# Attention's steps as one chain behind fixed products, its VectorE operations behind the unit's sums, its matmuls behind the last product

## The chip, the core and the metric

The kernel runs on one core of one Trainium2 chip. TensorE (PE) does the matmuls, VectorE (DVE), ScalarE (ACT) and GpSimd (POOL) the elementwise work, and SyncE (SP) issues the DMAs. The metric is the device time of the whole program in microseconds, as the median of several runs.

## The reference

Eight batches, eight heads, 576 tokens, head size 64. Each head has 32 packing queries p. First the packing queries attend to the keys and values, which gives 32 packed vectors per head; then every token's query attends to these, which serve as keys and values at once:

```
def sm_attn(qq, kk, vv):
    s = scale * np.matmul(qq, kk.transpose(0, 1, 3, 2))
    s = s - np.max(s, axis=-1, keepdims=True)
    a = np.exp(s)
    a = a / (np.sum(a, axis=-1, keepdims=True) + 1e-09)
    return np.matmul(a, vv)
p_packed = sm_attn(p, k, v)
out = sm_attn(q, p_packed, p_packed)
```

The result, 4608 tokens by 512, goes through four experts, all of which are computed for all tokens and weighted by the normalised domain probabilities:

```
p = domain_probs / (domain_probs.sum(-1, keepdims=True) + 1e-09)
for e in range(E):
    h = np.maximum(x @ w1[e], 0.0)       # 512 -> 1024
    out += p[:, e:e + 1] * (h @ w2[e])   # 1024 -> 512
```

## The kernel before

**Units.** The work of the experts is cut into 64 units: a super-block of two batches, one of eight chunks (512 hidden columns of an expert) and one of the two batches. A pair of units is the two batches of one chunk. The second layer of a unit is one Winograd form of a 2 x 2 block product: seven products instead of eight, in the order `ORDER` = a11, s3, s1, s2, a22, s4, a12, called products 0 to 6. Each product is 12 matmuls of 128 x 288 in float32r, since every operand is split into a high part (a cast on ScalarE, L102) and a low part (a subtraction, L107), and is added to an accumulator by VectorE (L420).

**First layer of the next unit.** The four blocks of hidden values of the next unit are made between the products of the current one: `mm1_group` (L294), 12 matmuls each, a11 behind product 1, a22 behind product 3, a21 behind product 4 and a12 behind product 6. VectorE then applies relu and the probability (L322) and forms the sums (L319): for a21 the operand s3, a sum in place, the operand s2, and ScalarE's copy s1 (L331); for a12 the operand s4, and ScalarE's and VectorE's split of a12 itself (stl). The other operands are split by ScalarE (hi) and GpSimd (lo) into tiles named st. These operations are called the sums below.

**x is never formed.** Instead, `g_form` (L259) multiplies the packed vectors (ppbd) by w1 once per chunk and super-block, 32 matmuls in every even unit behind products 2 and 3, and mm1_group multiplies the result (ghl) by the attention weights of the tokens (xh, xl).

**Attention** of the next super-block's two batches runs between the products of this one, in generators that do one step at each place given by `slots`. `pack_unit` (L139), once per half g of the heads: load k; load v; scores (32 matmuls into two tiles, issued together), maximum nb (L166, L167), exp on ScalarE (L170), its sum's reciprocal rs (L175, L176); then for each batch five transposes (L70) with ScalarE copies, 40 matmuls with v, the scaling ppn (L199), a transpose of ppn and its copies into ppbd. `tok_unit` (L212), once per g: load q; scores; transposes of the scores on VectorE (L225); for each batch maximum (L230), subtraction (L231), exp (L232), then sum (L235), 1e-9 (L236), reciprocal (L237), multiplication (L238), then transpose (L241) and split. `AT_FIRST` (super-block 0) and `AT_LATER` say at which unit of the super-block each of the four generators starts, and `slots` behind which products a step is taken: 0, 2, 4 and 6, or 0, 2 and 5 for the token side of super-block 0.

**What sets the order.** All matmuls of the kind above write to one pool of four tiles in PSUM, ps_dbl (two banks each, name dbl); a tile is free again when the last reader is done. Matmuls issued `together` (scores, g_form) are a fixed point in TensorE's order: all before stand before, all after stand after. Among everything else the tile framework's scheduler chooses the order on each engine from a simulation of the program as it is recorded. The engines then work their lists in order. The w2 operands (tt) are formed in super-block 0 from rw tiles by ScalarE and GpSimd (L393, t_form) and stored to DRAM, and are loaded from there later. The last super-block has no attention beside it.

## Time and profile before

| | |
|---|---|
| Median of 3 runs | 1309.03 us (1308.78 to 1310.23) |
| The profiled execution | 1306.86 us, of which its span 1304.8 us |
| TensorE busy | 1255.7 us, 96% |
| VectorE busy | 917.5 us, 70% |
| GpSimd busy | 732.6 us, 56% |
| ScalarE busy | 501.8 us, 38% |

The profiled execution is one run of its own, and the span begins and ends with the first and last instruction seen in it, so it is 2.06 us shorter than that run's time. A busy share is an average over a program with an opening, three super-blocks with attention and one without. In a timeline a row shows start and length of an instruction (or of several of one kind), its engine, line and operation, and in brackets how long the engine had been idle and what ended that; matmuls are pipelined, so rows overlap a little and a product of 12 shows 1.74 us where products follow each other every 1.58 us.

### The profile page before, as it was taken

Reading aid. Unit: us, or ns where it says so; the run is one execution under the profiler, and the core shown is the slowest. Engines: PE = TensorE matmul, PEld = TensorE weight load, DVE = VectorE, ACT = ScalarE, POOL = GpSimd, SP = SyncE. Lnnn points to the kernel's source line nnn. Section 1 sums busy time; section 2 is a strip of 40 time slices with the busy share of each in tenths; the row PEclk is TensorE's granted clock in tenths of the full one; section 3 lists DMA queues with packets and bytes.
Section 4 is the critical chain, followed back from the end, with each engine's and each line's share of the span. In section 5 each row is a group of like instructions: output and inputs, shape, how many; then the busy total and the mean of one; then the engine's idle time right before and its main releaser. Section 6 shows DMA issues by size and latency. Waiting matters only on the chain.

```text
span 1304.8 us, 26845 instructions
## 1 busy us (share of the span) xinstructions
PE 1255.7 (96%) x10720; PEld 1173.2 (90%) x10720; DVE 917.5 (70%) x1384; ACT 501.8 (38%) x841; POOL 732.6 (56%) x531
## 2 busy tenths in 40 slices
PE   5989998998999999999999999999999999999997
PEld 2879888898999989999999898999999999999997
DVE  6565666878784666887786566798678467766677
ACT  2444434344435333333334433343333543333331
POOL 4877768588774433445556443445546554345545
PEclk9999999999999999999999999999999999999999
DMA  9665656345455446454345644344445443345422
GB/s 340 235 230 181 223 200 219 127 165 198 155 195 171 151 135 191 160 175 139 121 143 184 208 143 153 127 154 155 140 138 192 150 137 122 126 155 155 123 65 74
DMA packets 86219, 213.71 MB, mean 164 GB/s; under 512 B 8784, under 2 KB 27344, under 8 KB 86096
## 3 DMA queue, kind: packets, MB, share of 16 engines
q1 hardware_dynamic: 85424, 211.85, 49.0%
q8 instruction: 86, 1.41, 0.4%
q14 instruction: 37, 0.30, 0.1%
q10 hardware_dynamic: 672, 0.15, 0.1%
HBM read 173.09 MB, written 38.87 MB: 162 GB/s over the span
## 4 chain that ended last, share of the span: by engine, by line
PE 83%; POOL 6%; DVE 4%; issue 2%; DMA 2%; ACT 2%; POOLq 0%; SPq 0%; DVEq 0%; ACTq 0%
PE dbl L67 78%; PE dbl L75 5%; POOL st L107 3%; POOL acc L470 1%; POOL tt L107 1%; DVE ghl L107 1%; PE dbl L70 1%; DMA wraw<-in_w 1%; ACT ghl L102 1%; DMA vt<-in_v 1%; DVE sblk L319 0%; DMA rw<-in_w 0%; DVE acc L435 0%; DVE acc L420 0%; DVE nb L166 0%
## 5 line engine op out<-in xcount | busy, mean ns | idle before, releaser
L67 PE MATMUL dbl<-st,tt 128*128 128x288 f32 x4608 | 669.3, 297 | 14.3 <-POOL st L107 9.3
L67 PEld LDWEIGHTS dbl<-st,tt 128*128 128x128 f32 x4608 | 625.3, 188 | 49.2 <-issue 26.5
L107 POOL TENSOR_TENSOR st<-sblk,st 128x576 fp32r<-128x576 f32 x256 | 371.9, 1463 | 426.6 <-ACT st L102 425.0
L67 PE MATMUL dbl<-xh,ghl 128*128 128x288 f32 x2048 | 416.3, 296 | 0.0
L420 DVE TENSOR_TENSOR acc<-dbl,acc 128x576 f32<-128x576 f32 x385 | 289.0, 751 | 103.0 <-PE dbl L67 101.9
L67 PEld LDWEIGHTS dbl<-xh,ghl 128*128 128x128 f32 x2048 | 331.0, 190 | 0.2 <-DVE ghl L107 0.2
L67 PE MATMUL dbl<-xl,ghl 128*128 128x288 f32 x1024 | 304.2, 297 | 6.8 <-POOL xl L107 5.3
L102 ACT CAST st<-sblk 128x576 fp32r<-128x576 f32 x256 | 166.5, 674 | 301.3 <-DVE sblk L319 232.1
L107 POOL TENSOR_TENSOR st<-ablk,st 128x576 fp32r<-128x576 f32 x128 | 184.2, 1439 | 64.9 <-ACT st L102 58.6
L67 PEld LDWEIGHTS dbl<-xl,ghl 128*128 128x128 f32 x1024 | 194.5, 190 | 9.4 <-POOL xl L107 6.0
L322 DVE SCALAR_TENSOR_TENSOR dbl<-dbl,pbt 128x576 f32<-128x576 f32 x128 | 97.9, 765 | 81.7 <-PE dbl L67 75.3
L102 ACT CAST st<-ablk 128x576 fp32r<-128x576 f32 x128 | 86.3, 674 | 159.1 <-PE dbl L67 141.4
L322 DVE SCALAR_TENSOR_TENSOR ablk<-dbl,pbt 128x576 f32<-128x576 f32 x128 | 96.5, 754 | 71.0 <-PE dbl L67 70.6
L67 PE MATMUL dbl<-stl,tt 128*128 128x288 f32 x768 | 114.6, 299 | 10.3 <-ACT sblk L331 8.8
L107 DVE TENSOR_TENSOR ghl<-dbl,ghl 128x512 fp32r<-128x512 f32 x128 | 85.4, 687 | 54.7 <-ACT ghl L102 54.7
L67 PEld LDWEIGHTS dbl<-stl,tt 128*128 128x128 f32 x768 | 106.7, 191 | 11.6 <-ACT sblk L331 9.7
L102 ACT CAST ghl<-dbl 128x512 fp32r<-128x512 f32 x128 | 72.0, 589 | 61.0 <-DVE ghl L107 47.5
L107 POOL TENSOR_TENSOR tt<-rw,tt 128x512 fp32r<-128x512 f32 x56 | 74.8, 1349 | 19.1 <-ACT tt L102 19.1
L75 PE MATMUL dbl<-wraw,ppbd 64*32 64x512 f32 x1024 | 68.2, 601 | 2.2 <-DMA wraw<-in_w 2.2
L107 DVE TENSOR_TENSOR stl<-dbl,stl 128x576 fp32r<-128x576 f32 x64 | 48.2, 754 | 30.6 <-ACT stl L102 30.4
L331 ACT COPY sblk<-dbl 128x576 f32<-128x576 f32 x64 | 41.0, 641 | 73.6 <-DVE sblk L319 65.7
L470 POOL TENSOR_TENSOR acc<-acc,acc 128x576 f32<-128x576 f32 x28 | 39.9, 1435 | 30.2 <-DVE acc L420 30.2
(65 smaller groups left out, 686.1 us busy)
## 6 DMA issues: line engine op xcount, KB each, us to landing
tt<-td SPq DMA_DIRECT2D x175, 512.0 KB, 4.1
wraw<-in_w SPq DMA_DIRECT2D x132, 256.0 KB, 3.7
td<-tt SPq DMA_DIRECT2D x56, 512.0 KB, 5.2
pbt<-pnd SPq DMA_DIRECT2D x32, 288.0 KB, 4.0
out<-acc SPq DMA_DIRECT2D x32, 288.0 KB, 2.6
rw<-in_w SPq DMA_DIRECT2D x16, 512.0 KB, 5.0
kt<-in_k SPq DMA_DIRECT2D x14, 576.0 KB, 4.7
kt<-in_q SPq DMA_DIRECT2D x14, 576.0 KB, 6.6
```

What stands on the lines that cost most here:

```text
L67: on_pe(nc.tensor.matmul(**kw))
L70: on_pe(nc.tensor.transpose(**kw))
L75: ins = nc.tensor.matmul(**kw).ins
L102: nc.scalar.copy(out=dst, in_=src)
L107: eng.tensor_tensor(out=dst, in0=src, in1=hi.bitcast(F32), op=ALU.subtract)
L322: nc.vector.scalar_tensor_tensor(out=held(name) if c == kh else psv, in0=psv, scalar=0.0, in1=pbt[b][:, ts].rearrange("p (o t) -> p o t", ...
L331: nc.scalar.copy(out=held("s1"), in_=psv)
L420: nc.vector.tensor_tensor(out=accs[b, i], in0=psv, in1=accs[b, i], op=ALU.add)
L470: eng.tensor_tensor(out=m[dst], in0=m[x], in1=m[y], op=op)
```

## The change

A small class `Behind` wraps VectorE. What goes through `vec` (the unit's sums, the split of a12, the final combination) is remembered as the last sum; what goes through `avec` (all of attention's VectorE operations) gets a dependency that keeps it behind the last sum recorded so far, in the order on the engine alone, with no semaphore. The accumulations (L420 before, L441 after) and the splits of ghl are not wrapped. In the same way `product` remembers its last matmul, and every matmul recorded later is kept behind it. Both hold from unit 1 on. The two tables are replaced by `pair_attention`, one chain of both pack units and both token units, each with a free place behind its loads, started at unit 4 of super-block 0 and unit 1 of a later one, counted from 0; a step stands behind products 0, 2 and 5 in odd units and 0, 3 and 5 in even ones. Line numbers of the changed kernel: L67 becomes L87, L75 L95, L70 L90, L107 L127, and all wrapped operations show the line of the wrapper, L68.

The diff, without the places where only nc.vector becomes vec or avec in the same way:

```
@@ -58,9 +58,29 @@
     def after(ins, prev):
         tc.add_manual_dep(ins, prev.name, nosync, reason="order on TensorE")
 
+    class Behind:
+
+        def __init__(self, eng, key):
+            self.eng, self.key, self.on = eng, key, False
+
+        def __getattr__(self, op):
+            def issue(*args, **kw):
+                res = getattr(self.eng, op)(*args, **kw)
+                if self.key is None:
+                    order["sum"] = res.ins
+                elif self.on and order["sum"] is not None:
+                    after(res.ins, order["sum"])
+                return res
+            return issue
+
+    order["sum"], order["product"] = None, None
+    vec, avec = Behind(nc.vector, None), Behind(nc.vector, "sum")
+
     def on_pe(res):
         if order["last"] is not None:
             after(res.ins, order["last"])
+        if avec.on and order["product"] is not None:
+            after(res.ins, order["product"])
         order["free"].append(res.ins)
 
     def mm(**kw):
@@ -163,8 +183,8 @@
         a1s, rss = {}, {}
         for b in bs:
             nb = small.tile([P, 1], F32, name="nb")
-            nc.vector.tensor_reduce(out=nb, in_=pss[b][:, :, 0:HS], axis=AX.XY, op=ALU.max)
-            nc.vector.tensor_scalar_mul(nb, nb, -SCALE)
+            avec.tensor_reduce(out=nb, in_=pss[b][:, :, 0:HS], axis=AX.XY, op=ALU.max)
+            avec.tensor_scalar_mul(nb, nb, -SCALE)
             a1s[b] = new(b, [P, S], "a1")
             sm = small.tile([P, 1], F32, name="sm")
             nc.scalar.activation(
...
@@ -222,23 +242,23 @@
             a2s[b] = new(b, [P, S // 32, NPK], "a1")
             a2f = a2s[b].rearrange("p a n -> p (a n)")
             for c in range(2):
-                nc.vector.transpose(out=a2f[:, c * HS:(c + 1) * HS], in_=pss[b][:, c, 0:HS])
+                avec.transpose(out=a2f[:, c * HS:(c + 1) * HS], in_=pss[b][:, c, 0:HS])
         yield
         for b in bs:
             a2 = a2s[b]
             m2 = small.tile([P, S // 32, 1], F32, name="m2")
-            nc.vector.tensor_reduce(out=m2, in_=a2, axis=AX.X, op=ALU.max)
+            avec.tensor_reduce(out=m2, in_=a2, axis=AX.X, op=ALU.max)
...
@@ -316,10 +336,10 @@
             return blocks[u, name]
 
         def add(dst, x, y, op):
-            nc.vector.tensor_tensor(out=dst, in0=x, in1=y, op=op)
+            vec.tensor_tensor(out=dst, in0=x, in1=y, op=op)
 
         name = f"a{c + 1}{kh + 1}"
-        nc.vector.scalar_tensor_tensor(
+        vec.scalar_tensor_tensor(
             out=held(name) if c == kh else psv, in0=psv, scalar=0.0,
             in1=pbt[b][:, ts].rearrange("p (o t) -> p o t", o=1).broadcast_to([P, 2, HS]),
             op0=ALU.max, op1=ALU.mult,
@@ -412,6 +432,7 @@
                         start=n == 0, stop=n == 5,
                     )
                     n += 1
+        order["product"] = order["free"][-1]
         psv = ps[:, :, 0:HS]
         if (b, i) not in accs:
             accs[b, i] = apool.tile([P, 2, HS], F32, name=f"acc{i}")
...
@@ -489,6 +510,16 @@
         for gen in gens:
             yield from gen
 
+    def pair_attention(pair):
+        for make in (pack_unit, tok_unit):
+            for g in range(NG):
+                gen = make(pair, g, att_tile)
+                next(gen)
+                if make is pack_unit:
+                    next(gen)
+                yield
+                yield from gen
+
     def drain(gen):
         for _ in gen:
             pass
...
@@ -566,13 +597,11 @@
     nothing = iter(())
     GROUPS = {1: ((0, 0),), 3: ((1, 1),), 4: ((0, 1),), 6: ((1, 0),)}
     GROUPS_LATE = {3: ((0, 0),), 4: ((1, 1),), 5: ((0, 1),), 6: ((1, 0),)}
-    AT_FIRST = ((4, pack_unit, 0), (6, pack_unit, 1), (8, tok_unit, 0), (11, tok_unit, 1))
-    AT_LATER = ((1, pack_unit, 0), (4, pack_unit, 1), (7, tok_unit, 0), (9, tok_unit, 1))
     FORM = {0: (0, 2, 3, 4, 5, 6), 2: (6,), 3: (0, 1, 2, 3, 4)}
     for kh in range(2):
         w2_load(1, kh, raw_tile)
     tsteps = nothing
-    sums, back, slots = nothing, second_batch(), (0, 1, 2, 3, 4, 5, 6)
+    sums, back = nothing, second_batch()
     for u, (sb, ch, b) in enumerate(units):
         pos = u % (2 * NCH)
         odd = pos % 2 == 1
@@ -581,13 +610,11 @@
 
         if u == 1:
             drain(back)
-        if sb + 1 < SB:
-            pair = [2 * sb + 2, 2 * sb + 3]
-            for at_step, make, g in AT_FIRST if sb == 0 else AT_LATER:
-                if at_step == pos:
-                    drain(back)
-                    back = make(pair, g, att_tile)
-                    slots = (0, 2, 5) if sb == 0 and make is tok_unit else (0, 2, 4, 6)
+            avec.on = True
+        if sb + 1 < SB and pos == (4 if sb == 0 else 1):
+            drain(back)
+            back = pair_attention([2 * sb + 2, 2 * sb + 3])
+        slots = range(NPROD) if u == 0 else (0, 2, 5) if odd else (0, 3, 5)
 
         gsteps, gat = nothing, (2, 3)
         nsb, nch = (sb, ch + 1) if ch + 1 < NCH else (sb + 1, 0)
```

**VectorE, the second scores of super-block 1.** Unit 20, before. nb belongs to attention's pack unit; SCALAR_TENSOR_TENSOR is relu with the probability, here of a21; sblk are s3 and s2; acc are accumulations.

```order
L322 SCALAR_TENSOR_TENSOR dbl<-dbl,pbt 128x2x288
L319 TENSOR_TENSOR sblk<-ablk,dbl 128x576
L319 TENSOR_TENSOR dbl<-dbl,ablk 128x2x288
L166 TENSOR_REDUCE nb<-dbl 128x1 x2
L319 TENSOR_TENSOR sblk<-dbl,ablk 128x576
L167 TENSOR_SCALAR nb<-nb 128x1 x2
L420 TENSOR_TENSOR acc_4835<-dbl,acc_4835 128x576
L175 TENSOR_SCALAR rs<-sm 128x1
L176 RECIPROCAL rs<-rs 128x1
L175 TENSOR_SCALAR rs<-sm 128x1
L176 RECIPROCAL rs<-rs 128x1
L420 TENSOR_TENSOR acc_4855<-dbl,acc_4855 128x576
```

Afterwards, at the same scores:

```order
L68 SCALAR_TENSOR_TENSOR dbl<-dbl,pbt 128x2x288
L68 TENSOR_TENSOR sblk<-ablk,dbl 128x576
L68 TENSOR_TENSOR dbl<-dbl,ablk 128x2x288
L441 TENSOR_TENSOR acc_5097<-dbl,acc_5097 128x576
L68 TENSOR_TENSOR sblk<-dbl,ablk 128x576
L441 TENSOR_TENSOR acc_5126<-dbl,acc_5126 128x576
L68 SCALAR_TENSOR_TENSOR dbl<-dbl,pbt 128x2x288
L68 TENSOR_TENSOR sblk<-dbl,sblk 128x576
L441 TENSOR_TENSOR acc_4660<-dbl,acc_4660 128x576
L68 TENSOR_TENSOR stl<-dbl,stl 128x2x288
L68 TENSOR_REDUCE nb<-dbl 128x1 x2
L68 TENSOR_SCALAR nb<-nb 128x1 x2
```

The maximum nb, which stood between the sums of a21, now stands behind the sums of a21 and of a12, with stl the last of them.

**TensorE, the same scores.** Before: kt is the operand of the scores, xl and xh those of the group a21, st and stl those of products 5 and 6.

```order
L67 MATMUL dbl<-xl_2773,ghl 128x288
L67 MATMUL dbl<-xh_2772,ghl 128x288 x2
L75 MATMUL dbl<-kt,pt 32x288 x16
L67 MATMUL dbl<-st,tt 128x288 x12
L67 MATMUL dbl<-stl,tt 128x288 x12
L67 MATMUL dbl<-xl_2773,ghl 128x288
L67 MATMUL dbl<-xh_2772,ghl 128x288 x2
```

Afterwards:

```order
L87 MATMUL dbl<-xl_3065,ghl 128x288
L87 MATMUL dbl<-xh_3064,ghl 128x288 x2
L87 MATMUL dbl<-st,tt 128x288 x12
L95 MATMUL dbl<-kt,pt 32x288 x16
L87 MATMUL dbl<-st,tt 128x288 x12
L87 MATMUL dbl<-xl_3069,ghl 128x288
L87 MATMUL dbl<-xh_3068,ghl 128x288 x2
```

In unit 20 the scores stood between group a21 (of unit 21) and product 5; now they stand between products 0 and 1, which follow group a12 of unit 20 itself.

**VectorE, the token side in super-block 0.** Before: a, s and at are attention's (two batches, a_2874 and a_2877), the others the unit's.

```order
L235 TENSOR_REDUCE s_3047<-a_2874 128x18
L322 SCALAR_TENSOR_TENSOR dbl<-dbl,pbt 128x2x288
L235 TENSOR_REDUCE s_3263<-a_2877 128x18
L420 TENSOR_TENSOR acc_838<-dbl,acc_838 128x576
L236 TENSOR_SCALAR s_3047<-s_3047 128x18
L319 TENSOR_TENSOR sblk<-ablk,dbl 128x576
L319 TENSOR_TENSOR dbl<-dbl,ablk 128x2x288
L236 TENSOR_SCALAR s_3263<-s_3263 128x18
L420 TENSOR_TENSOR acc_870<-dbl,acc_870 128x576
L237 RECIPROCAL s_3047<-s_3047 128x18
L322 SCALAR_TENSOR_TENSOR dbl<-dbl,pbt 128x2x288
L319 TENSOR_TENSOR sblk<-dbl,ablk 128x576
```

Afterwards:

```order
L68 TENSOR_REDUCE s_3369<-a_3185 128x18
L441 TENSOR_TENSOR acc_790<-dbl,acc_790 128x576
L68 TENSOR_SCALAR s_3369<-s_3369 128x18
L68 RECIPROCAL s_3369<-s_3369 128x18
L68 TENSOR_TENSOR a_3185<-a_3185,s_3369 128x576
L68 SCALAR_TENSOR_TENSOR dbl<-dbl,pbt 128x2x288
L68 TENSOR_TENSOR sblk<-ablk,dbl 128x576
L68 TENSOR_TENSOR dbl<-dbl,ablk 128x2x288
L441 TENSOR_TENSOR acc_838<-dbl,acc_838 128x576
L68 TENSOR_TENSOR sblk<-dbl,ablk 128x576
L68 STREAM_TRANSPOSE at<-a_3185 128x576
L441 TENSOR_TENSOR acc_870<-dbl,acc_870 128x576
```

Small operations of two batches stood between the unit's sums; now one batch's operations stand in a row ahead of a group's sums or behind them.

## Rows read from the trace of the kernel before

**Rows 1.** The page: busy us, share, instructions; issues: KB each, us to landing.
```profile
PE 1255.7 (96%) x10720; PEld 1173.2 (90%) x10720; DVE 917.5 (70%) x1384; ACT 501.8 (38%) x841; POOL 732.6 (56%) x531
...
kt<-in_q SPq DMA_DIRECT2D x14, 576.0 KB, 6.6
```

**Rows 2.** Stretches: window, length, busy PE, PEld, DVE, ACT, POOL, PEclk, DMA share, GB/s.
```profile
137.76:390.32 252.56, 238.24 (x2090) 222.53 (x2089) 187.74 (x284) 105.93 (x180) 188.22 (x138) 0.99 0.52 180
390.32:703.20 312.88, 309.27 (x2682) 291.27 (x2681) 225.28 (x344) 118.73 (x198) 154.56 (x109) 0.99 0.49 160
703.20:1016.15 312.95, 309.32 (x2681) 291.33 (x2680) 225.31 (x344) 118.74 (x198) 154.49 (x109) 0.99 0.48 154
1052.99:1089.82 36.83, 36.83 (x297) 35.28 (x297) 25.74 (x36) 12.51 (x20) 16.95 (x12) 1.00 0.43 138
515.59:553.75 38.16, 38.16 (x330) 35.81 (x329) 32.29 (x53) 14.46 (x23) 15.38 (x11) 1.00 0.49 164
665.67:703.20 37.53, 37.11 (x298) 35.33 (x297) 31.20 (x40) 13.59 (x22) 25.88 (x18) 1.00 0.56 190
484.00:487.40 3.40, 3.40 (x17) 3.40 (x17) 1.07 (x5) 2.21 (x6) 1.68 (x2) 0.56 0.20 64
```

**Rows 3.** Timeline of PE in unit 17: start, length, instruction, [idle before <-releaser].
```profile
423.06 0.71 PE L70 MATMUL dbl<-ident,a 128*128 128x128 f32 x5
...
427.80 0.29 PE L67 MATMUL dbl<-xl,ghl 128*128 128x288 f32 x1
...
432.93 0.30 PE L70 MATMUL dbl<-ident,ppn 128*64 128x128 f32 x1
432.98 1.83 PE L67 MATMUL dbl<-st,tt 128*128 128x288 f32 x12
```

**Rows 4.** Timeline of PE: five of the waits, 177 to 484 us.
```profile
177.90 0.30 PE L70 MATMUL dbl<-ident,ppn 128*64 128x128 f32 x1 [1.15 <-DVE ppn L199]
...
233.70 1.81 PE L67 MATMUL dbl<-st,tt 128*128 128x288 f32 x12 [1.10 <-DVE ghl L107]
...
252.18 1.85 PE L67 MATMUL dbl<-st,tt 128*128 128x288 f32 x12 [1.44 <-POOL st L107]
...
309.45 3.25 PE L67 MATMUL dbl<-st,tt 128*128 128x288 f32 x12 [3.56 <-POOL st L107]
...
483.68 3.25 PE L67 MATMUL dbl<-stl,tt 128*128 128x288 f32 x12 [2.20 <-ACT sblk L331]
```

**Rows 5.** Timeline of DVE in unit 20, behind the scores of pack unit 1.
```profile
480.82 1.41 DVE L166 TENSOR_REDUCE nb<-dbl 128x1 f32<-128x576 f32 x2
482.15 0.75 DVE L319 TENSOR_TENSOR sblk<-dbl,ablk 128x576 f32<-128x576 f32 x1
```

**Rows 6.** Timeline of ACT at the same place in unit 20.
```profile
482.98 0.64 ACT L331 COPY sblk<-dbl 128x576 f32<-128x576 f32 x1 [1.97 <-DVE nb L167]
483.52 0.75 ACT L170 ACTIVATE a<-dbl,nb 128x576 f32<-128x576 f32 x1
```

**Rows 7.** Timeline of ACT in a unit without attention.
```profile
1102.03 0.64 ACT L331 COPY sblk<-dbl 128x576 f32<-128x576 f32 x1 [1.30 <-DVE sblk L319]
```

**Rows 8.** Timeline of PE at the same place as rows 7.
```profile
1102.86 3.32 PE L67 MATMUL dbl<-st,tt 128*128 128x288 f32 x24
```

**Rows 9.** Timeline of POOL ahead of the wait at 309.45.
```profile
306.25 1.26 POOL L393 TENSOR_TENSOR rw<-rw,rw 128x512 f32<-128x512 f32 x1 [1.54 <-DMA rw<-in_w]
307.47 1.93 POOL L107 TENSOR_TENSOR st<-sblk,st 128x576 fp32r<-128x576 f32 x1
```

**Rows 10.** Timeline of DVE: two multiplies of the token side.
```profile
250.87 1.88 DVE L238 TENSOR_TENSOR a<-a,s 128x576 f32<-128x576 f32 x1
...
548.86 0.70 DVE L238 TENSOR_TENSOR a<-a,s 128x576 f32<-128x576 f32 x1
```

**Rows 11.** Timeline of POOL beside the first of them.
```profile
250.73 3.31 POOL L107 TENSOR_TENSOR st<-sblk,st 128x576 fp32r<-128x576 f32 x2
```

**Rows 12.** Groups of DVE: count, busy us, mean ns, idle before.
```profile
L238 DVE TENSOR_TENSOR a<-a,s 128x576 f32<-128x576 f32 x16 | 19.1, 1194 | 0.0
```

More of the change, by code (lines that the diff above doesn't have):

```diff
@@ L59, in after, with __init__, __getattr__, issue @@
         tc.add_manual_dep(ins, prev.name, nosync, reason="order on TensorE")
+    class Behind:
+        def __init__(self, eng, key):
+            self.eng, self.key, self.on = eng, key, False
+        def __getattr__(self, op):
+            def issue(*args, **kw):
+                res = getattr(self.eng, op)(*args, **kw)
+                if self.key is None:
+                    order["sum"] = res.ins
+                elif self.on and order["sum"] is not None:
+                    after(res.ins, order["sum"])
+                return res
+            return issue
+    order["sum"], order["product"] = None, None
+    vec, avec = Behind(nc.vector, None), Behind(nc.vector, "sum")
     def on_pe(res):
@@ L63, in on_pe @@
             after(res.ins, order["last"])
+        if avec.on and order["product"] is not None:
+            after(res.ins, order["product"])
         order["free"].append(res.ins)
@@ L198, in pack_unit @@
             ppn = small.tile([P, D], F32, name="ppn")
-            nc.vector.tensor_scalar_mul(ppn, ps[:, 0, 0:D], rss[b])
+            avec.tensor_scalar_mul(ppn, ps[:, 0, 0:D], rss[b])
             yield
@@ L224, in tok_unit @@
             for c in range(2):
-                nc.vector.transpose(out=a2f[:, c * HS:(c + 1) * HS], in_=pss[b][:, c, 0:HS])
+                avec.transpose(out=a2f[:, c * HS:(c + 1) * HS], in_=pss[b][:, c, 0:HS])
         yield
@@ L240, in tok_unit @@
             a2t = new(b, [P, S], "at")
-            nc.vector.transpose(out=a2t, in_=a2.rearrange("p a n -> p (a n)"))
+            avec.transpose(out=a2t, in_=a2.rearrange("p a n -> p (a n)"))
             xh, xl = (t[:, g, :, 0:HS] for t in xs[b])
@@ L414, in product @@
                     n += 1
+        order["product"] = order["free"][-1]
         psv = ps[:, :, 0:HS]
@@ L490, in chain, with pair_attention @@
             yield from gen
+    def pair_attention(pair):
+        for make in (pack_unit, tok_unit):
+            for g in range(NG):
+                gen = make(pair, g, att_tile)
+                next(gen)
+                if make is pack_unit:
+                    next(gen)
+                yield
+                yield from gen
     def drain(gen):
@@ L574, in attention_moe @@
     tsteps = nothing
-    sums, back, slots = nothing, second_batch(), (0, 1, 2, 3, 4, 5, 6)
+    sums, back = nothing, second_batch()
     for u, (sb, ch, b) in enumerate(units):
@@ L583, in attention_moe @@
             drain(back)
-        if sb + 1 < SB:
-            pair = [2 * sb + 2, 2 * sb + 3]
-            for at_step, make, g in AT_FIRST if sb == 0 else AT_LATER:
-                if at_step == pos:
-                    drain(back)
-                    back = make(pair, g, att_tile)
-                    slots = (0, 2, 5) if sb == 0 and make is tok_unit else (0, 2, 4, 6)
+            avec.on = True
+        if sb + 1 < SB and pos == (4 if sb == 0 else 1):
+            drain(back)
+            back = pair_attention([2 * sb + 2, 2 * sb + 3])
+        slots = range(NPROD) if u == 0 else (0, 2, 5) if odd else (0, 3, 5)
         gsteps, gat = nothing, (2, 3)
```

46 lines of the change are left out of this document (22 added, 24 removed).

## The prediction

> **What bounds the kernel now.** I read the page's busy shares first: TensorE is busy 96% of the span and VectorE 70% [rows 1], so what can be gained here is time in which TensorE stands or runs slowly. Then the table of stretches [rows 2], because the average hides where that time is. I cut the span at the g_form step, once per pair of units. A pair in the last super-block, where no attention runs, lasts 36.83 us with TensorE busy for all of it. The three stretches in which attention of the next two batches runs are the three earlier super-blocks: 252.56 us for 6 pairs, 312.88 and 312.95 us for 8 pairs each. Over clean pairs that is 252.56 - 6 x 36.83 = 31.6 us, 312.88 - 8 x 36.83 = 18.2 and 18.3 us: 68.1 us together. This is all that the change can touch: order and work after 1016 us stay, and so do the first 140 us.
>
> Not all of the 68.1 us is waiting. A pair that holds one scores step and none of TensorE's other attention work lasts 38.16 us [rows 2], so 32 score matmuls for two batches cost 38.16 - 36.83 = 1.33 us. Per batch a pack unit further has five transposes, 40 small matmuls against v and one transpose of ppn: from 423.06 to 427.80 stand the first two with two products of 1.58 us each [rows 3], which leaves 4.74 - 3.16 = 1.58, and the ppn transpose adds about 0.1 (432.93 to 432.98), so 1.7. A super-block has two pack units (1.33 + 2 x 1.69 = 4.7 each) and two token units (1.33 each): 12.1 us, 36.2 us in three. The last pair of a super-block, with combine, lasts 37.53 instead of 36.83, 2.1 us in three. What is left is waiting and slow clock: 68.1 - 36.2 - 2.1 = **29.8 us**, of which 18.8 in super-block 0 and 5.5 in each of the other two.
>
> The timeline of TensorE names most of it [rows 4]. Four times (two in super-block 0, one in each later one; the row at 483.68 is one) a product waits 2.20 us on ScalarE's copy into sblk: 8.8 us. Twice it waits 1.15 us for ppn: 2.3. Once each in super-block 0: 3.56 and 1.44 on GpSimd's st, 1.10 on VectorE's ghl. The product behind the waits at 309.45 and 483.68 takes 3.25 us where one takes 1.85 behind other waits, 1.4 more: in the stretch behind 483.68 the granted clock is 0.56 [rows 2], near the lower of the two levels (1.2 of 2.4 GHz), after TensorE had stood for 2.2 us. Four of the five longest waits are followed by such a stretch (the one at 198.06 us is not): 4 x 1.4 = 5.6 us. These sum to 22.8; the other 7.0 us are many short waits.
>
> **The change part by part.** *VectorE behind the sums.* The 2.20 us is made like this [rows 5, 6]: the maximum for the softmax (nb, two operations, 1.41 us) starts on VectorE at 480.82, ahead of the subtraction s2, which therefore starts at 482.15; ScalarE's copy s1 follows at 482.98 and ends at 483.62, and only then is the tile of PSUM that held a21 free; the product starts at 483.68. In the clean pair [rows 7, 8] the same copy ends at 1102.67 and the product that needs a tile begins at 1102.86: a margin of 0.2 us, which the 1.41 us of nb exceeds by 1.2, and the rest of the wait is the delay of the sums before it. After the change nb stands behind all sums of the group, and the scores stand where no a21 is in work (behind products 0, 2, 3 and 5). All four waits and their slow products go: 8.8 + 3 x 1.4 = 13.0 us. If the cover were gone, each would come back at 2.20 + 1.4 = 3.6.
>
> *What is late next.* The four tiles of PSUM are shared, so the two that scores take are held until ScalarE's exp (pack) or VectorE's transposes (token). At a place behind product 0 VectorE still has sums of a12 in hand for about 1.6 us after the scores begin, then nb 1.41 and 0.20, then exp 0.75 [rows 5, 6]: 4.0 to 4.5 us, against 1.13 + 2 x 1.58 = 4.3 until the second product behind the scores needs the first tile: a wait of 0 to 0.25, I take 0.25. At a place behind product 5 a token step's scores last 1.13 us, and product 6 wants the tile of product 5, whose accumulation ends about 1.6 us after it: a wait of 0.45. The places behind 2 and 3 fit. One of each kind per super-block: 0.7, three times 2.1 us.
>
> *Matmuls behind the last product.* Transposes, v products and ppn transposes each now stand behind a whole product of 1.58 us. The 1.15 us for ppn is VectorE's scaling of a tile that the v matmuls have just written; a product in between covers it, and 2.3 us go. The price of the cover gone is 1.15 each.
>
> *Token steps in super-block 0.* The 1.44 at 252.18 and the 1.10 at 233.70 come from two batches' sums, reciprocals and multiplies among the unit's own sums on VectorE. As one chain they come one batch at a time and behind the sums: 2.5 us go. The 3.56 at 309.45 has another cause [rows 9]: GpSimd waits 1.54 us for a load of w2 (rw), subtracts, and the st for the next product starts only at 307.47. In the changed order both st operands of this place stand ahead of that subtraction. I take it as gone with its slow product (3.56 + 1.4 = 5.0); if the order stands but w2's load comes as late at another st, it stays.
>
> *Loads.* The loads are issued by SyncE. A q load lands 6.6 us after issue (the page's median) [rows 1]. In unit 22 the step that issues it stands only three groups (4.7 us) before its scores, but in SyncE's order it stands ahead of the w1 loads that the same unit's g_form needs, and g_form stands five groups (5 x 1.58 = 7.9 us) before the scores, so it is covered; a k load has a step of its own ahead of the scores as before. Cost 0, at worst 6.6 - 4.7 = 1.9 at two places.
>
> *What stays.* The long waits with their slow products, 22.8 us, all go by the parts above. Of the short waits (7.0 us) I let half stay, 3.5, since part of them hang on ghl, on the first accumulation and on w2's loads and not on attention. Sum: 29.8 - 2.1 - 3.5 = **24.2 us** gone. The profiled execution took 1306.86 us, 2.17 under the median of the runs; 1306.86 - 24.2 = 1282.7 there, **1284.8** as a median. Bounds: all waits gone is 1309.03 - 29.8 = 1279.2.
>
> *GpSimd and VectorE.* Attention's multiplies on VectorE (a by s, both in SBUF) last 0.70 us at 548.86, with GpSimd idle, and 1.88 at 250.87, where GpSimd's two st run from 250.73 on [rows 10, 11]; the mean of 16 is 1.19 [rows 12]; the subtractions are operations of the same size. The change puts them behind the sums, which is where GpSimd's st come too. Twelve of each move: at most about 24 x (1.88 - 1.19) = 16.6 us more on VectorE, at least nothing. In the pair at 515.59 VectorE is busy 32.29 of 38.16 us without holding TensorE, so I count 0 and keep the rest for the range.
> The Trainium skill, "SBUF — State Buffer", section "Who interferes with whom", says that VectorE and GpSimd share one port pair as an exclusive lock: whichever operation starts first holds it to its end. The trace agrees, with 0.70 against 1.88. By that rule alone each moved operation would meet st and VectorE would be the one that is late, which is the upper end of case (a) below; by the busy shares it stays hidden.
>
> **Rivals.** *(a) Half the gain.* GpSimd and VectorE decide super-block 0: the waits on st and ghl stay (3.56 + 1.4 + 1.44 + 1.10 = 7.5 us): 1292.3. With the slower multiplies of that super-block (a third of 16.6, 5.5 us) on the path as well: 1297.8. For it: there GpSimd is busy 188 of 252 us and VectorE 188 [rows 2]. Against: the later super-blocks have no such waits, and the order moves the st.
> *(b) Slower: sums first starve the tiles.* Scores hold two of four tiles, and their release now waits behind every sum that is already recorded. Its point is the margin above, -0.25 and -0.45 us: once VectorE is later than that by a further microsecond at a scores step, TensorE stops long enough to fall to the lower clock, and each of the 12 scores steps costs 2.2 + 1.4 = 3.6: 43.2 - 29.8 = 13.4 us more, 1322. For it: two thin margins. Against: at products 0 to 3 VectorE has idle time in the clean pair (25.74 of 36.83).
> *(c) The waits only move.* The same PSUM tiles and the same operations, another order, equal waiting: 1309. Against: VectorE's rows do change at the very place of the 2.20.
>
> **How the numbers follow.** The forecast has 0.68 (1279 to 1290), (a) 0.18 (1290 to 1300), (c) 0.06, (b) 0.08. About 0.2%, 2.6 us, is what a measurement here tells from no change. Faster: 0.68 + 0.18 + 0.01 of (c) = 0.87; same 0.05; slower 0.08. The range takes in the forecast and (a): 1279 to 1300.
>
> **What would show it.** In the changed profile the three stretches together lose about 24 us of their 68 us over clean pairs, of which some 14 in super-block 0. TensorE has no 2.20 wait on ScalarE's sblk and no 1.15 wait on ppn, and no product of 3.25 us. On VectorE s2 follows a21's sum with at most an accumulation between, and nb follows stl. New waits, if any, are of 0.2 to 0.5 behind scores, on ScalarE's a or VectorE's acc. I am wrong if TensorE waits over 1 us behind scores for nb or a (b), or if st still holds super-block 0 (a).

## The result, and the profile after

The changed kernel takes **1291.03 us** (median of 4 runs, 1290.36 to 1291.79) against 1308.9 us (1308.43 to 1310.23) before: a ratio of 0.9866, 95% interval 0.985 to 0.9881. The prediction was 1284.8 us in a range of 1279 to 1300: faster, as forecast, with 17.9 us of the 24.2 that it had worked out. It lies in the part of that range (1290 to 1300) that the prediction gave to its rival (a).

The profiled execution took 1291.5 us, and its page shows the same work with less standing: TensorE busy 1252.9 instead of 1255.7 us [rows 1], over a span 15.1 us shorter.

```profile
span 1289.7 us, 26846 instructions
...
PE 1252.9 (97%) x10720; PEld 1169.5 (91%) x10720; DVE 925.2 (72%) x1384; ACT 498.1 (39%) x841; POOL 732.7 (57%) x531
```

The stretches of the three super-blocks, cut again at the first g_form of each [rows 2] (the fourth row is the g_form behind the longest wait):

```profile
140.91:384.65 243.74, 237.79 (x2089) 219.92 (x2089) 185.90 (x284) 104.31 (x180) 187.91 (x138) 0.99 0.54 186
384.65:692.90 308.25, 307.45 (x2682) 289.76 (x2681) 230.18 (x344) 117.81 (x198) 154.72 (x109) 1.00 0.50 163
692.90:1001.10 308.20, 307.40 (x2681) 289.71 (x2680) 230.16 (x344) 117.81 (x198) 154.73 (x109) 1.00 0.49 156
...
306.17:309.40 3.23, 3.23 (x34) 0.74 (x33) 1.28 (x2) 1.26 (x2) 3.23 (x4) 0.59 0.09 12
```

Against 252.56, 312.88 and 312.95 that is 8.8, 4.6 and 4.8 us, 18.2 together. The span shows only 15.1, because the stretch began 3.15 us later (140.91 instead of 137.76). The g_form before it already stands at 108.62 instead of 105.43, where every engine still has the same order of instructions in both kernels; behind the third stretch both take 288.6 us. So the two profiled executions differ in their opening, ahead of the change's first effect, and below I compare stretches and not single profiles' spans.

What TensorE waits for in the changed kernel (timeline; start, length, instruction, idle before and its releaser):

```profile
202.13 1.82 PE L87 MATMUL dbl<-st,tt 128*128 128x288 f32 x12 [0.30 <-DVE nb L68]
...
222.38 1.84 PE L87 MATMUL dbl<-st,tt 128*128 128x288 f32 x12 [0.48 <-POOL st L127]
...
271.55 1.82 PE L87 MATMUL dbl<-st,tt 128*128 128x288 f32 x12 [0.84 <-DVE ghl L127]
...
304.06 2.18 PE L87 MATMUL dbl<-st,tt 128*128 128x288 f32 x12 [1.97 <-POOL st L127]
306.17 3.23 PE L95 MATMUL dbl<-wraw,ppbd 64*32 64x512 f32 x32
...
364.31 1.84 PE L87 MATMUL dbl<-st,tt 128*128 128x288 f32 x12 [0.57 <-DVE stl L68]
...
367.07 1.85 PE L87 MATMUL dbl<-st,tt 128*128 128x288 f32 x12 [0.92 <-POOL st L127]
...
516.40 1.85 PE L87 MATMUL dbl<-stl,tt 128*128 128x288 f32 x12 [0.34 <-DVE acc L441]
```

Against [rows 4]: the 2.20 on ScalarE's sblk is gone at all four places, the 1.15 on ppn at both. The new waits behind scores are 0.30 (202.13, once) and 0.34 (516.40, once per super-block). What is left stands in super-block 0, above all 1.97 us on GpSimd's st, with a g_form behind it that takes 3.23 us instead of 1.95, at a granted clock of 0.59. On VectorE, at the scores of [rows 5], nb now follows stl:

```profile
459.76 0.76 DVE L68 TENSOR_TENSOR stl<-dbl,stl 128x576 fp32r<-128x576 f32 x1 [0.54 <-ACT stl L122]
460.44 1.41 DVE L68 TENSOR_REDUCE nb<-dbl 128x1 f32<-128x576 f32 x2
```

And the token side's operations [rows 12] have become longer, the multiplication from 1.19 to 1.34 us in the mean, the subtraction from 0.83 to 1.10 (means of 16, of which four belong to the opening):

```profile
L68 DVE TENSOR_TENSOR a<-a,s 128x576 f32<-128x576 f32 x16 | 21.4, 1336 | 0.4
L68 DVE TENSOR_TENSOR a<-a,m 128x576 f32<-128x576 f32 x16 | 17.6, 1099 | 0.1
```

### The profile page after: what moved, and what is told of

Read it like the earlier page. It is cut to its first block, busy times and chain, and to the rows that moved or that the text cites. A ratio compares the mean times of both kernels' runs of the same rounds, so it can differ in the third digit from the quotient of the medians.

```text
span 1289.7 us, 26846 instructions
## 1 busy us (share of the span) xinstructions
PE 1252.9 (97%) x10720; PEld 1169.5 (91%) x10720; DVE 925.2 (72%) x1384; ACT 498.1 (39%) x841; POOL 732.7 (57%) x531
## 4 chain that ended last, share of the span: by engine, by line
PE 83%; POOL 6%; DVE 5%; issue 2%; ACT 2%; DMA 1%; POOLq 0%; SPq 0%; DVEq 0%; ACTq 0%
PE dbl L87 77%; PE dbl L95 5%; POOL st L127 3%; POOL acc L491 1%; POOL tt L127 1%; PE dbl L90 1%; DVE a L68 1%; DMA rw<-in_w 1%; DVE acc L68 1%; DVE ghl L127 1%; DVE acc L441 1%; DVE dbl L68 0%; ACT st L122 0%; POOL rw L413 0%; DVE nb L68 0%
## 5 line engine op out<-in xcount | busy, mean ns | idle before, releaser
L87 PE MATMUL dbl<-st,tt 128*128 128x288 f32 x4608 | 667.8, 296 | 12.3 <-POOL st L127 7.1
L87 PEld LDWEIGHTS dbl<-st,tt 128*128 128x128 f32 x4608 | 624.4, 188 | 49.3 <-issue 26.6
L127 POOL TENSOR_TENSOR st<-sblk,st 128x576 fp32r<-128x576 f32 x256 | 372.4, 1464 | 392.5 <-ACT st L122 365.6
L87 PE MATMUL dbl<-xh,ghl 128*128 128x288 f32 x2048 | 415.5, 296 | 0.0
L441 DVE TENSOR_TENSOR acc<-dbl,acc 128x576 f32<-128x576 f32 x385 | 289.2, 752 | 90.5 <-PE dbl L87 87.3
L87 PEld LDWEIGHTS dbl<-xh,ghl 128*128 128x128 f32 x2048 | 329.9, 189 | 0.2 <-DVE ghl L127 0.2
L87 PE MATMUL dbl<-xl,ghl 128*128 128x288 f32 x1024 | 303.5, 296 | 8.7 <-POOL xl L127 7.3
L127 POOL TENSOR_TENSOR st<-ablk,st 128x576 fp32r<-128x576 f32 x128 | 185.0, 1445 | 59.2 <-ACT st L122 57.0
L87 PEld LDWEIGHTS dbl<-xl,ghl 128*128 128x128 f32 x1024 | 193.7, 189 | 11.2 <-POOL xl L127 8.1
L68 DVE SCALAR_TENSOR_TENSOR dbl<-dbl,pbt 128x576 f32<-128x576 f32 x128 | 97.8, 764 | 82.9 <-PE dbl L87 75.8
L68 DVE SCALAR_TENSOR_TENSOR ablk<-dbl,pbt 128x576 f32<-128x576 f32 x128 | 96.4, 753 | 54.0 <-PE dbl L87 53.4
L127 DVE TENSOR_TENSOR ghl<-dbl,ghl 128x512 fp32r<-128x512 f32 x128 | 85.3, 688 | 54.0 <-ACT ghl L122 53.8
L87 PE MATMUL dbl<-stl,tt 128*128 128x288 f32 x768 | 113.0, 296 | 1.0 <-DVE acc L441 1.0
L87 PEld LDWEIGHTS dbl<-stl,tt 128*128 128x128 f32 x768 | 104.5, 188 | 3.2 <-DVE acc L441 2.6
L127 POOL TENSOR_TENSOR tt<-rw,tt 128x512 fp32r<-128x512 f32 x56 | 73.6, 1331 | 18.0 <-ACT tt L122 17.9
L68 DVE TENSOR_TENSOR stl<-dbl,stl 128x576 fp32r<-128x576 f32 x64 | 48.4, 756 | 38.7 <-ACT stl L122 38.7
L95 PE MATMUL dbl<-wraw,ppbd 64*32 64x512 f32 x1024 | 69.0, 606 | 0.0
L439 ACT COPY acc<-dbl 128x576 f32<-128x576 f32 x56 | 35.9, 641 | 51.5 <-PE dbl L87 51.3
```

What stands on the lines that cost most here:

```text
L68: res = getattr(self.eng, op)(*args, **kw)
L87: on_pe(nc.tensor.matmul(**kw))
L95: ins = nc.tensor.matmul(**kw).ins
L127: eng.tensor_tensor(out=dst, in0=src, in1=hi.bitcast(F32), op=ALU.subtract)
L439: nc.scalar.copy(out=accs[b, i], in_=psv)
L441: nc.vector.tensor_tensor(out=accs[b, i], in0=psv, in1=accs[b, i], op=ALU.add)
```

## The experiments

All stretches in one table, from g_form to g_form as above, each from one profiled execution. A ratio is to the kernel before, run on the same chip; the medians of before were 1305.4 to 1308.9 in these series.

| kernel | ratio (95%) | super-block 0 | 1 | 2 |
|---|---|---|---|---|
| before | 1 | 252.56 | 312.88 | 312.95 |
| changed | 0.9866 (0.985-0.9881) | 243.74 | 308.25 | 308.20 |
| chain_only | 0.988 (0.9847-0.9913) | 244.75 | 308.52 | 308.50 |
| chain_vec | 0.9862 (0.9834-0.989) | 244.70 | 308.25 | 308.26 |
| chain_pe | 0.9879 (0.9847-0.991) | 242.78 | 308.50 | 308.50 |
| old_places | 1.0028 (1.0012-1.0045) | 249.91 | 315.47 | 315.19 |
| old_nb | 0.9937 (0.9914-0.9959) | 248.65 | 310.96 | 311.04 |
| form_late | 0.9857 (0.9831-0.9883) | 242.74 | 308.26 | 308.24 |
| no_mult | 0.9835 (0.9808-0.9861) | 238.45 | 308.19 | 308.18 |
| cast_behind | 0.9837 (0.9816-0.9859) | 240.80 | 308.25 | 308.24 |
| cast_pe | 0.9893 (0.9871-0.9916) | 248.93 | 308.54 | 308.55 |
| one_input | 0.9851 (0.9831-0.987) | 242.15 | 308.18 | 308.20 |
| cast_late | **0.9819** (0.9802-0.9836) | 238.37 | 308.26 | 308.23 |
| one_place | 0.9918 (0.9897-0.994) | 248.60 | 308.50 | 308.50 |

Three of these kernels are one and the same in their order. In the profiles of the changed kernel, chain_vec and form_late every engine has the same instructions in the same order over these stretches, and so have chain_only and chain_pe. So the table shows how far executions of one order differ: 2.0 us in super-block 0 (242.74 to 244.70, and 242.78 to 244.75), less than 0.1 us in the other two.

### Which part of the change gains: the places or the rules

Two theories stood against each other. Theory P: the new places gain, since no scores stand behind a21. Theory V: the rule that puts attention's VectorE operations behind the sums gains. Four kernels take the change apart. chain_only has both rules off:

```
-                elif self.on and order["sum"] is not None:
+                elif False and order["sum"] is not None:
...
-        if avec.on and order["product"] is not None:
+        if False and order["product"] is not None:
```

> The changed kernel with both rules off: the chain at its new places stays, VectorE's attention operations and TensorE's matmuls are ordered by the scheduler alone. Theory P (the places are the gain: no scores behind a21, so nothing can delay the copy s1): about 1291, within 3 us of the changed kernel. Theory V (the rule on VectorE is the gain: without it nb and the token operations stand among the sums again): 1300 to 1310, with waits of 1 to 2 us on ScalarE's sblk or on st. The ppn transposes may wait 1.15 again in either, 2 to 4 us in all.

chain_vec has only the second of these edits (TensorE's rule off), chain_pe only the first (VectorE's rule off).

> The changed kernel without the rule on TensorE; the rule on VectorE and the places stay. If the rule on TensorE only covers ppn (1.15 us at two places of the kernel before), 1291 to 1294. If it also keeps transposes and v matmuls from standing in a row, more waits of about 1 us appear at up to 12 places: up to 1303.

> The changed kernel without the rule on VectorE; the rule on TensorE and the places stay. Theory P: 1291 plus or minus 3. Theory V: 1300 or more, and the lost time stands in waits on VectorE's and GpSimd's operands, mostly in super-block 0 where VectorE is busiest. Together with the run that has both rules off it tells what each rule is worth alone.

old_places keeps both rules and takes back tables, start units and slots:

```
-        if sb + 1 < SB and pos == (4 if sb == 0 else 1):
-            drain(back)
-            back = pair_attention([2 * sb + 2, 2 * sb + 3])
-        slots = range(NPROD) if u == 0 else (0, 2, 5) if odd else (0, 3, 5)
+        if sb + 1 < SB:
+            pair = [2 * sb + 2, 2 * sb + 3]
+            for at_step, make, g in AT_FIRST if sb == 0 else AT_LATER:
+                if at_step == pos:
+                    drain(back)
+                    back = make(pair, g, att_tile)
+                    slots = (0, 2, 5) if sb == 0 and make is tok_unit else (0, 2, 4, 6)
```

> Both rules, but the places and the start units of the kernel before (two tables, steps behind products 0, 2, 4 and 6). The pack scores stand behind the group a21 again. Theory P: the waits of 2.2 us stay in part, since nb still comes before the sums of a12 and holds two tiles: 1300 to 1309. Theory V: nb no longer delays s2, the 2.2 us go: 1290 to 1295. The slower rival of the prediction (tiles starved) would give over 1309 here first.

Measured: the three stretches took 878.39 us before. With VectorE's rule off they take 861.77 (chain_only) and 859.78 (chain_pe), with it on 860.19 (changed), 861.21 (chain_vec) and 859.24 (form_late, below). So the new places and the chain, which these runs take together, give 16.6 to 18.6 us, nearly all of the gain; no run parts the two. VectorE's rule gives 0.25 us in each later super-block, and in super-block 0 nothing that stands out from the 2.0 us between executions. TensorE's rule changes no engine's order here, so it is worth nothing at these places. The times of the four kernels with the new places can't be told apart by their intervals either. At the old places the two rules make the kernel 0.3% slower, which is over what either theory had said. Theory P holds, theory V falls.

One row could be taken for a price of TensorE's rule. In chain_vec the second pair takes 43.34 us instead of 41.82, and a ppn transpose waits 1.67 us. The rows (VectorE, GpSimd, ScalarE, TensorE) show another cause:

```profile
208.90 0.28 DVE L68 TENSOR_SCALAR ppn<-dbl,rs 128x64 f32<-128x64 f32 x1
...
211.74 1.29 POOL L413 TENSOR_TENSOR rw<-rw,rw 128x512 f32<-128x512 f32 x1 [3.78 <-DMA rw<-in_w]
...
213.06 0.62 ACT L122 CAST tt<-rw 128x512 fp32r<-128x512 f32 x1 [5.32 <-POOL rw L413]
213.59 0.63 ACT L351 COPY sblk<-dbl 128x576 f32<-128x576 f32 x1
...
214.27 0.30 PE L90 MATMUL dbl<-ident,ppn 128*64 128x128 f32 x1 [1.67 <-ACT sblk L351]
```

ppn was ready 5 us earlier. The transpose waits for ScalarE's copy s1, which stands behind a cast of w2's operand, and that cast waits for GpSimd's rw and a load of w2. This load landed 7.7 us after its issue, against 6.1 us in the changed kernel. In the other executions in which ScalarE, GpSimd and SyncE have the same lists up to there, the second pair goes the same way: 41.44 and 41.57 us where it took 5.7 and 5.9 (form_late, chain_pe), 43.34 and 42.98 where it took 7.7 and 7.3 (chain_only and one_input, below).

At the old places VectorE's rule has a price, in old_places; first TensorE, then VectorE:

```profile
180.62 0.42 PE L90 MATMUL dbl<-ident,ppn 128*64 128x128 f32 x1 [3.12 <-DVE ppn L68]
```

```profile
179.62 0.76 DVE L68 TENSOR_TENSOR stl<-dbl,stl 128x576 fp32r<-128x576 f32 x1 [1.21 <-ACT stl L122]
180.29 0.27 DVE L68 TENSOR_SCALAR ppn<-dbl,rs 128x64 f32<-128x64 f32 x1
```

ppn, whose input had long been there (the v matmuls ended near 177.5), stands behind the last sum of a12, and TensorE waits 3.12 us where it waited 1.15 [rows 4]. That is rival (b) in kind, a release that waits for sums, but at ppn and not at the scores.

### What makes the 2.20 us

old_nb is the kernel before with nb alone behind the sums recorded so far (places and tables of before, all else without rules):

```
-            nc.vector.tensor_reduce(out=nb, in_=pss[b][:, :, 0:HS], axis=AX.XY, op=ALU.max)
-            nc.vector.tensor_scalar_mul(nb, nb, -SCALE)
+            avec.tensor_reduce(out=nb, in_=pss[b][:, :, 0:HS], axis=AX.XY, op=ALU.max)
+            avec.tensor_scalar_mul(nb, nb, -SCALE)
```

> The kernel before with one edit: only the two operations of nb (the maximum and its scaling) are kept behind the last sum recorded; places, tables and everything else as before. If nb ahead of s2 makes the 2.20 us waits, the four waits shrink by about nb's 1.4 us each, to 0.8 or less, and their slow stretches go: 4 x 1.4 + 3 x 1.4 = 9.8 us, about 1299. If the held tiles make them, they stay at about 2 us and the time stays at 1309, or rises, as the scores' tiles are held longer.

one_place goes the other way: chain_only with one scores step put behind a21.

```
-        slots = range(NPROD) if u == 0 else (0, 2, 5) if odd else (0, 3, 5)
+        slots = range(NPROD) if u == 0 else (0, 2, 5) if odd else (0, 4, 6) if u == 4 else (0, 3, 5)
```

> The changed kernel with both rules off and one scores step moved: in unit 4 the steps stand behind products 0, 4 and 6 instead of 0, 3 and 5, so that the first pack scores of super-block 0 stand behind the group a21 and nb comes ahead of s2 on VectorE. If place and nb make the 2.20 us wait, it is back there and there alone: 2.20 on ScalarE's copy into sblk, with or without 1.4 of slow clock behind it, and the first pair takes 43.6 to 45 instead of 41.42 us. If the place does not matter, it stays at 41.4.

In one_place the wait is back there and there alone; TensorE, then VectorE:

```profile
154.15 2.50 PE L87 MATMUL dbl<-stl,tt 128*128 128x288 f32 x12 [2.19 <-ACT sblk L351]
```

```profile
150.63 0.76 DVE L68 TENSOR_TENSOR dbl<-dbl,ablk 128x576 f32<-128x576 f32 x1
151.30 1.41 DVE L68 TENSOR_REDUCE nb<-dbl 128x1 f32<-128x576 f32 x2
152.63 0.75 DVE L68 TENSOR_TENSOR sblk<-dbl,ablk 128x576 f32<-128x576 f32 x1
```

nb stands between the sum and s2, as in [rows 5]. The first pair takes 45.43 us instead of 41.42, so 4.0 us for one place (the prediction's price was 2.20 + 1.4 = 3.6); the other five pairs of super-block 0 agree with chain_only within 0.2 us. In old_nb, with s2 ahead of nb, the same wait has halved and has no slow stretch behind it:

```profile
477.74 1.85 PE L87 MATMUL dbl<-stl,tt 128*128 128x288 f32 x12 [1.08 <-ACT sblk L351]
```

```profile
476.20 0.76 DVE L68 TENSOR_TENSOR sblk<-dbl,ablk 128x576 f32<-128x576 f32 x1
476.87 1.41 DVE L68 TENSOR_REDUCE nb<-dbl 128x1 f32<-128x576 f32 x2
```

I had expected 0.8 or less and 9.8 us; it was 1.07 and 1.08 at these four places, a wait of 0.73 elsewhere became 1.42 to 1.50, and the stretches gained 7.7 us. old_places, which also has s2 ahead of nb, shows 1.07 or 1.08 at the same four places, with no slow product either. So nb's place makes about half of the wait, and without that half no slow stretch followed; the other half, which goes with the place, fits the scores holding two of the four tiles, so that a21's tile is wanted sooner than in the clean pair [rows 7, 8]. That half was not measured by itself.

### What holds super-block 0

The changed kernel's wait of 1.97 us at 304.06 is the largest left. ScalarE ahead of it, then GpSimd:

```profile
299.27 0.62 ACT L122 CAST tt<-rw 128x512 fp32r<-128x512 f32 x1 [2.20 <-DMA rw<-in_w]
299.80 0.67 ACT L122 CAST xh<-at 128x576 fp32r<-128x576 f32 x1
300.37 1.24 ACT L122 CAST st<-sblk 128x576 fp32r<-128x576 f32 x2
```

```profile
299.97 1.29 POOL L127 TENSOR_TENSOR tt<-rw,tt 128x512 fp32r<-128x512 f32 x1 [1.36 <-ACT tt L122]
301.23 1.41 POOL L127 TENSOR_TENSOR xl<-at,xh 128x576 fp32r<-128x576 f32 x1
302.61 1.40 POOL L127 TENSOR_TENSOR st<-sblk,st 128x576 fp32r<-128x576 f32 x1
```

ScalarE's list has a cast of w2's operand at its head, which waits 2.20 us for the load of w2, and behind it stand a cast of xh and the casts of st that the next products need. GpSimd's list has the same order. form_late records the steps that form w2's operands later:

```
-        form_at = FORM.get(u, () if fch is None else (1, 2, 3, 4) if odd else (1, 4))
+        form_at = FORM.get(u, () if fch is None else (1, 2, 3, 4) if odd else (3, 5))
```

> The changed kernel with the two steps that form w2's operands in even units of super-block 0 moved from behind products 1 and 4 to behind 3 and 5. If the wait of 1.97 us at 304.06 comes from ScalarE's cast that stands waiting for w2's load ahead of the casts of st, it goes, with its slow stretch (1.3 us): 3 us faster, about 1288. If GpSimd's total load is the cause, the wait only moves to another st: 1291 or slower.

The wait stayed (2.10 us at 303.73), since every engine's list came out as in the changed kernel: what was recorded later was put at the same place. So it tested nothing about the queue. The 1.0 us that super-block 0 took less is a difference between two executions of one order; in this one the g_form behind the wait took 1.95 us, at a granted clock of 1.00. no_mult takes VectorE's part out (result of batches 2 to 7 changed, as its expectation says):

```
-            eng.tensor_tensor(out=a2, in0=a2, in1=m2.broadcast_to([P, S // 32, NPK]), op=ALU.subtract)
+            if order.get("opening"):
+                eng.tensor_tensor(out=a2, in0=a2, in1=m2.broadcast_to([P, S // 32, NPK]), op=ALU.subtract)
...
-            eng.tensor_tensor(out=a2, in0=a2, in1=s2.broadcast_to([P, S // 32, NPK]), op=ALU.mult)
+            if order.get("opening"):
+                eng.tensor_tensor(out=a2, in0=a2, in1=s2.broadcast_to([P, S // 32, NPK]), op=ALU.mult)
```

> The changed kernel without the token side's subtraction and multiplication on VectorE for batches 2 to 7 (left out; the result of these batches is not the reference's). It takes 24 operations of 1.1 to 1.3 us, some 29 us, from VectorE and takes away the sharing of their time with GpSimd's st. If that sharing and VectorE's load hold super-block 0 (rival a), 4 to 7 us go there: 1284 to 1287. If w2's load and the order of ScalarE hold it, under 1 us goes: 1290 to 1291.

Super-block 0 went down by 5.3 us against the changed kernel's profile (4.3 to 6.3 against the three executions of its order), and the wait at 304 vanished. This fits rival (a), but a second cause could hide behind it: with VectorE early, what ScalarE waits for comes early too. cast_behind acts on that queue alone: each cast of tt is kept, in ScalarE's order, behind the last cast of st.

```
-                hi_of(t[:, 0], blk[of[name]], hi_eng)
+                ins = hi_of(t[:, 0], blk[of[name]], hi_eng)
+                if avec.on:
+                    after(ins, order["cast"])
...
-        hi_of(st[:, 0], src, nc.scalar)
+        order["cast"] = hi_of(st[:, 0], src, nc.scalar)
```

> The changed kernel, with each cast on ScalarE that forms a w2 operand (tt) kept behind the last cast of an st recorded before it. At the wait of 304.06 ScalarE's cast of tt stood 2.20 us for w2's load, ahead of two casts of st, and GpSimd's low part of tt stood ahead of its st. If that queue makes the wait, 1.97 us shrink to 0.7 or less (GpSimd's xl, 1.4 us, still stands ahead of the st) and the g_form behind it runs at 1.95 instead of 3.23: the six pairs of super-block 0 take 241 instead of 243.7 us, about 1288. If VectorE's lateness makes it (the run without subtraction and multiplication), the wait stays near 2 and only moves: 243 to 244, about 1291.

The pair with the wait (the fourth) fell from 41.31 to 38.17 us and the fifth from 39.43 to 38.16, with VectorE's load unchanged; the first pair rose from 41.42 to 43.47, with a new wait of 1.26 us on GpSimd's tt at 147.25. So the queue makes that wait, which stood at 1.91 to 2.10 us in all three executions of the changed order. cast_late applies the rule from unit 8 on only (`if order["late"]`, set by `u >= 8`, in place of `if avec.on`):

> The changed kernel with ScalarE's casts of tt kept behind the last cast of st from unit 8 on only. With the rule from unit 1 on the fourth pair of super-block 0 went from 41.31 to 38.17 us and the fifth from 39.43 to 38.16, but the first from 41.42 to 43.47. If these are separate, the first pair stays at 41.4 and super-block 0 takes about 239 us: 1286, against 1291 for the changed kernel and 1288 for the rule from unit 1 on. If the first pair's cost only moves on, 241 and 1288.

The two effects are separate: the first pair is at 41.43, the fourth at 38.21, super-block 0 at 238.37 us, 4.4 to 6.3 less than in the three executions of the changed order. The second pair is at 40.63, although its load of w2 took 7.4 us: the copy s1 no longer stands behind the cast. In cast_late's trace, at the place of the former wait, ScalarE's two st casts and GpSimd's st now stand ahead of tt, and no wait is left:

```profile
293.85 1.24 ACT L122 CAST st<-sblk 128x576 fp32r<-128x576 f32 x2
295.00 0.61 ACT L122 CAST tt<-rw 128x512 fp32r<-128x512 f32 x1
```

```profile
295.42 2.83 POOL L126 TENSOR_TENSOR st<-sblk,st 128x576 fp32r<-128x576 f32 x2
298.20 1.29 POOL L126 TENSOR_TENSOR tt<-rw,tt 128x512 fp32r<-128x512 f32 x1
```

With 1283.68 us (1282.79 to 1285.12) and 0.9819 it is the fastest of all, its interval clear of the changed kernel's (those of chain_vec and form_late touch it). cast_pe joins the cast rule (from unit 1) with VectorE's rule off:

> The same rule for ScalarE, and the rule on VectorE off. Of the runs so far the one without VectorE's rule has the shortest super-block 0 (242.8 us). If both add, super-block 0 takes 240 to 241 us and the kernel 1287 to 1288; if they act on the same wait, 242 to 243 and 1290.

The two do not add: super-block 0 took 248.93 us, since in this order TensorE waits 4.09 us for VectorE's ghl at 274.27. The two rules together give the scheduler another list, and another wait comes with it.

one_input keeps the operations but not their second input (no_mult's edit, with this line in place of each operation left out):

```
+            else:
+                eng.tensor_scalar_mul(a2, a2, 0.5)
```

> The changed kernel with the token side's subtraction and multiplication of batches 2 to 7 replaced by a multiplication by 0.5 in place: the same count and size, but one input in SBUF and a constant (so these batches' results are not the reference's). If the two operations cost because they and GpSimd's st wait for each other (0.70 alone, 1.1 to 1.3 in the mean), they fall to 0.4 to 0.7 us and super-block 0 comes near the 238.5 us of the run without them: 1286. If it is VectorE's load as such, about half of that gain is seen: 241 us, 1288. If such an operation still meets GpSimd, its mean stays over 1 us and nothing changes.

```profile
L68 DVE TENSOR_SCALAR a<-a 128x576 f32<-128x576 f32 x24 | 16.3, 678 | 0.0
```

The mean of 0.68 us is made of two kinds. 17 of the 24 last 0.45 us; the other seven, which overlap with GpSimd's operations, last 0.83 to 1.74:

```profile
276.19 0.45 DVE L68 TENSOR_SCALAR a<-a 128x576 f32<-128x576 f32 x1
...
327.24 1.74 DVE L68 TENSOR_SCALAR a<-a 128x576 f32<-128x576 f32 x1
```

```profile
325.83 1.43 POOL L127 TENSOR_TENSOR st<-ablk,st 128x576 fp32r<-128x576 f32 x1
327.23 1.43 POOL L127 TENSOR_TENSOR st<-sblk,st 128x576 fp32r<-128x576 f32 x1
328.62 1.51 POOL L419 TENSOR_TENSOR rw<-rw,rw 128x512 f32<-128x512 f32 x1
```

At 276.19 GpSimd is idle. So an operation with one input still meets GpSimd, and it is shorter by itself as well (0.45 against the 0.70 of [rows 10]): the edit changed both, and can't tell the lengthening from VectorE's load. Super-block 0 took 242.15 us, only 0.6 less than the shortest execution of the changed order, with a wait of 1.30 us in the second pair, where the load of w2 came late (7.3 us). How much of what no_mult gains is the lengthening stays open.

## Why the prediction was right, and where not

**Right: the reading of the three stretches.** What is waiting and what is attention's own work was told apart well enough: the later super-blocks were forecast to lose about 10 us together and lost 9.4; they are at 308.2, with under 1 us of waits left in each.

**Right in mechanism, wrong in owner: "VectorE behind the sums".** The four waits of 2.20 us and their slow stretches went, and nb ahead of s2 is the mechanism (one_place: 4.0 us for one place, forecast 3.6). But the step that takes them away is the place of the scores; the rule that names the change gives 0.25 us in each later super-block beside it, and at the old places, together with TensorE's, these waits halve but others grow (ppn).

**Right: "What is late next".** Forecast 0.25 behind product 0 and 0.45 behind product 5 in each super-block, 2.1 us; measured 0.30 once and 0.34 in each, 1.3 us. Rival (b) did not happen here. Its price supposed a slow stretch behind a wait about a microsecond longer than these; [rows 4] has 1.44 us with a product of 1.85 behind it, and in old_nb the products behind 1.42 and 1.50 took 1.85 too.

**Right in effect, but not by the rule: "Matmuls behind the last product".** The two waits of 1.15 us for ppn went, 2.3 us as forecast. They are gone without the rule as well (chain_only, chain_vec), in the same order on TensorE: the new places already put a product between.

**The step that failed: "Token steps in super-block 0", with the 3.56 us "taken as gone".** The prediction wanted some 14 us there and 8.8 came (7.9 and 9.8 in the other two executions of this order); that is nearly all of the miss of 6.0 us between 24.2 and 18.2. It looked at the order of st and of the subtraction of w2 on GpSimd, and both st did move ahead. It did not follow ScalarE's list, where a cast waits for the load of w2 with the casts of st behind it. The wait came back as 1.97 us plus a slow product (2.18 instead of 1.85) and a slow g_form (3.23 instead of 1.95): 3.6 of the 5.0 us. In the other two executions it came back as 1.91 and 2.10, with no slow stretch. The text had the condition, a load as late at another st, but gave it no share in the sum. cast_late removes it, and 5.4 us of super-block 0 with it: 4.4 in the fourth and fifth pairs and 1.2 in the second, less 0.2 in the third. The rest is in waits of 0.5 to 0.9 (271.55, 364.31, 367.07). Two of them are on VectorE's ghl and on GpSimd's st, like the 1.10 and 1.44 that this step also took as gone.

By the prediction's own sign, st still holding super-block 0, this is rival (a), and the time lies where it said. Its cause was only in part the one that it gave, what GpSimd and VectorE have to do: less work for VectorE takes the wait away (no_mult), but so does another order of ScalarE's list and of the lists that follow it, with the same work on both engines (cast_late).

**The lengthened multiplications.** Bounded at 16.6 us of VectorE time and counted at 0; without the operations super-block 0 is 4.3 to 6.3 us shorter, and the others the same. That this is near the 5.5 that rival (a) put on the path is a coincidence, since no_mult leaves out whole operations and not their lengthening. This gain is not added to cast_late's: both take away the wait at 304. The Trainium skill, "SBUF — State Buffer", section "Who interferes with whom", says that an operation of VectorE with two SBUF inputs contends with a GpSimd instruction that reads SBUF, and lists `tensor_scalar` among those that can do so in a mode that takes both port pairs. The trace agrees that both kinds are held up here (0.70 against 1.88 us with two inputs [rows 10], 0.45 against 1.74 with one); by which port no run shows.

## What to carry to other kernels

An operation that holds shared tiles belongs where no chain of sums is about to release one: the place did here what a rule of order was meant to do, and at the old places the rules made things worse. Before a wait is taken as gone, follow the lists of all engines that feed it: one cast that waits for a load holds up every cast queued behind it, and an order that was set for one engine leaves that on another. Compare stretch by stretch, since two executions can differ by more in their opening than an edit is worth; and compare the engines' lists before an edit is given a price, since two edits here changed no list, and stretches of one order differed by 2 us.

## What the runs showed of the hardware

The opening varies between executions: up to the first g_form of the compared stretch the profiles of before, the changed kernel, chain_vec and old_places took 137.76, 140.91, 135.34 and 141.19 us. In the first two the difference is there at 105 us, where their orders are still the same on every engine; the changed kernel and chain_vec, 5.6 us apart, have the same order throughout. What makes it was not settled. One load of w2, issued at the same point, landed after 5.7 to 7.7 us, and the pair of units that needs it took 41.4 to 43.3 us with it. A wait of the same length is not always followed by a lower clock: TensorE stood for 2.20 us at four places of the kernel before and was slow behind three of them, not behind the one at 198.06; in the changed kernel 1.97 us at 304.06 were followed by a g_form at 0.59, and at the same place of the same order 1.91 us (chain_vec) and 2.10 us (form_late) were followed by a granted clock of 1.00. In old_places 3.12 us for ppn were followed by a granted clock of 0.50, 2.78 us for the next ppn by 1.00. What decides it was not settled.
